# Attention and feed-forward kernel on one core: pooled value sums on TensorE for the first sequence, an earlier exp table, moved casts, ordered waits and a new plan

## Chip, cores and metric

One Trainium2 chip, one core. The metric is the device time of one execution in microseconds (us); of the kernel before, three runs were timed. A program of this kind is a set of five instruction streams that wait for each other through semaphores: TensorE (PE in the profile, its weight loads PEld), VectorE (DVE), ScalarE (ACT), GpSimd (POOL) and SyncE (SP), which here only issues transfers.

## What is computed

Eight sequences of 576 tokens, eight heads of 64. The reference, cut to what matters:

```python
def sm_attn(qq, kk, vv):                       # softmax(q k^T / 8) v
    s = scale * np.matmul(qq, kk.transpose(0, 1, 3, 2))
    a = np.exp(s - np.max(s, axis=-1, keepdims=True))
    return np.matmul(a / (np.sum(a, axis=-1, keepdims=True) + 1e-09), vv)
q_d, k_d, v_d = (mean over groups of 4 tokens of q, k, v)        # 144 pooled tokens
out_up = np.repeat(sm_attn(q_d, k_d, v_d), 4, axis=2)
out_local = the same attention over all 576 tokens, masked to |i - j| < 4
x = (out_up + out_local) as 4608 x 512
h = x @ w_in                                   # 512 x 2048
out = np.maximum(0.01 * h, h) @ w_out          # 2048 x 512
```

The products of the feed-forward part keep fp32 precision: each operand is split into a high and a low part of a shorter type (fp32r), and three matmuls (high by high, high by low, low by high) are summed.

## The kernel before

**Stages.** The 4608 tokens are cut into ten chunks of up to 512 columns. The first sequence is done on its own at the start, with its local attention on TensorE; the other seven sequences' local attention runs on POOL and DVE while TensorE works on the feed-forward products of the chunks that are there. Heads go in pairs, so a sequence has four channels c = 0 to 3 of 128 partitions.

- *Start, first sequence* (`pooled`, `vsums`, `vrest`, `windows`, `banded` with batch 0). Per channel: `given` loads q and k (qk); the pooled q and k (qk_d) are sums of four, by one DVE reduce (L525) or by two POOL additions (L519, L521; channels 1 and 2); TensorE multiplies them (L543), DVE takes the maximum (L555), ACT the exp (L561). `vsums` reduces the loaded v (su_vs) by four on DVE to su_vd (L445); L635 multiplies it with the weights. `banded` does the local part in two halves hf of the sequence (256 and 320 tokens): scores into a PSUM tile (L814), DVE maximum, subtraction and sum (L821, L822, L827), ACT exp (L825) and sum plus 1e-9 (L829), POOL scaling (L833), TensorE transposes (L841), ACT copy (L843), TensorE values (L856); DVE adds the pooled result, each column four times (L867), and ACT and DVE split the sum into x high and low (L879, L881). When all four channels of the first half are there, TensorE's feed-forward matmuls can begin.
- *Weights* (`convert`): every 128x512 piece of w_in and w_out is cast (L374 on ACT), repaired by a two-input DVE operation (L376), and split into high (L383 on ACT) and low (L386 on POOL or L389 on DVE, by a string of flags). It uses the prod tiles and, in the start, pieces of x1 (x in the rows).
- *Feed-forward*: `up_proj` (L1118, hp), `leaky` (ACT L1139 and L1140, DVE L1142: gh and gl), `down_proj` (L1164, acc). 
- *Other sequences*: per piece two POOL products of 128x1344 (scores L944, values L1020), each reduced by DVE (L950, L1026), then `landing` transposes and adds (L1042, L1050) into x. Pooled attention of these: `pooled` and `duo` (L688, L710).
- *Late chunks*: the last three are parked in DRAM and read back. `fetched`, `combine_x` and `split_t` read them into the output buffer (olot) and split or combine them with the two-input helper `both` (L1239); the last two chunks go through a Strassen scheme (`finale`, L1419).

**Order.** `Order` holds generators, each spawned with a rank. It repeatedly takes the operation that can start first by its own model of the engines (`COST`, a model of the transfers in `wire`), ties and near ties going by rank, and so writes the order of every engine's program, which then is fixed. Nothing overtakes on an engine. `staging`, `swap` and `cleared` open and close the buffers of the start; `busy` puts filler matmuls on TensorE where the plan has gaps (L342, L347, L355). `load` (L273) issues every transfer on SP.

**Two-input operations.** An operation of DVE with `lock` is planned behind what POOL has; `held` notes it, and `behind` adds a wait to a POOL operation that follows within 31.4 us of the plan:

```python
def held(ins):
    od.held = ins, od.engine["DVE"]
def behind(ins):
    first, end = od.held
    if first is not None and od.engine["POOL"] - end < NEAR:
        tc.add_manual_dep(ins.ins, first.ins.name, ...)
```

## Time and profile before

| | |
|---|---|
| median of three runs | 892.03 us (891.53 to 893.36) |
| the profiled execution | 893.24 us, its span 891.5 us |
| mean granted clock of TensorE | 0.993 |
| busy: PE, DVE, ACT, POOL | 872.8 us (98%), 639.4 (72%), 461.4 (52%), 628.9 (71%) |
| HBM traffic | 119.67 MB, 134 GB/s |
| chain that ended last | PE 86%, DVE 6%, DMA 4%, ACT 3% |

How to read it: the span is the profile's time from the first to the last record, the execution's own time lies 1.7 us around it. Busy shares are averages over stages; the view by stretches tells them apart. A row of the trace's groups gives line, engine, operation, tiles (out<-in), partitions x elements, xcount, the busy time and mean duration, and behind the last bar the idle time of the engine just before them with what ended it. In a timeline the columns are start, duration, engine, line, operation, and in brackets the idle time before it and what ended it.

### The profile page before, as it was taken

Reading aid. Unit: us, or ns where it says so; the run is one execution under the profiler, and the core shown is the slowest. Engines: PE = TensorE matmul, PEld = TensorE weight load, DVE = VectorE, ACT = ScalarE, POOL = GpSimd, SP = SyncE. Lnnn points to the kernel's source line nnn. Section 1 sums busy time; section 2 is a strip of 40 time slices with the busy share of each in tenths; the row PEclk is TensorE's granted clock in tenths of the full one; section 3 lists DMA queues with packets and bytes.
Section 4 is the critical chain, followed back from the end, with each engine's and each line's share of the span. In section 5 each row is a group of like instructions: output and inputs, shape, how many; then the busy total and the mean of one; then the engine's idle time right before and its main releaser. Section 6 shows DMA issues by size and latency. Waiting matters only on the chain.

```text
span 891.5 us, 13603 instructions
## 1 busy us (share of the span) xinstructions
PE 872.8 (98%) x4815; PEld 721.1 (81%) x4815; DVE 639.4 (72%) x952; ACT 461.4 (52%) x1288; POOL 628.9 (71%) x316
## 2 busy tenths in 40 slices
PE   6999999999999999999999999999999999999998
PEld 3687878988899888887888888778878888888886
DVE  5888989888896988898788977887786443323322
ACT  3898866656463744466345635623443244435421
POOL 3434478798999899999998899889976433374000
PEclk9999999999999999999999999999999999999999
DMA  9878764555453563455455535534344000000001
GB/s 336 278 234 293 241 187 133 191 167 186 140 154 111 180 189 113 139 160 171 119 148 174 171 107 160 158 100 116 115 113 137 3 24 24 1 1 1 24 24 48
DMA packets 67684, 119.67 MB, mean 134 GB/s; under 512 B 8608, under 2 KB 34720, under 8 KB 67616
## 3 DMA queue, kind: packets, MB, share of 16 engines
q1 hardware_dynamic: 67616, 118.80, 42.9%
q8 instruction: 38, 0.62, 0.3%
q14 instruction: 30, 0.25, 0.1%
HBM read 106.19 MB, written 12.58 MB: 133 GB/s over the span
## 4 chain that ended last, share of the span: by engine, by line
PE 86%; DVE 6%; DMA 4%; ACT 3%; issue 1%; SPq 0%; POOL 0%; DVEq 0%; POOLq 0%; ACTq 0%
PE acc L1164 35%; PE hp L1118 32%; PE hp L1419 4%; PE pt L1419 4%; DMA qk<-in_qkt_dram 3%; PE hp L1164 2%; PE pt L1164 2%; PE pt L688 1%; DVE xloc L1026 1%; PE pt L707 1%; PE pt L751 1%; DMA stage<-in_w_out_dram 1%; PE pt L710 1%; ACT x L374 1%; DVE gl L1142 0%
## 5 line engine op out<-in xcount | busy, mean ns | idle before, releaser
L1118 PE MATMUL hp<-x,wi 128*128 128x512 f32 (+2 forms) x1632 | 333.7, 356 | 4.1 <-DVE gl L1142 4.1
L1118 PEld LDWEIGHTS hp<-x,wi 128*128 128x128 f32 x1632 | 277.2, 189 | 45.6 <-DVE gl L1142 7.5
L1020 POOL TENSOR_TENSOR prod<-v,sx 128x1344 f32<-128x1344 f32 x84 | 264.3, 3148 | 29.3 <-DVE xloc L1026 16.8
L944 POOL TENSOR_TENSOR prod<-q,k 128x1344 f32<-128x1344 f32 x84 | 261.5, 3114 | 27.4 <-DVE wi L389 8.8
L1164 PE MATMUL acc<-woh,gh 128*128 128x512 f32 x512 | 202.4, 395 | 0.0
L1164 PE MATMUL acc<-wol,gh 128*128 128x512 f32 x512 | 199.9, 390 | 0.0
L1164 PE MATMUL acc<-woh,gl 128*128 128x512 f32 x512 | 199.8, 390 | 0.0
L1139 ACT ACTIVATE gh<-hp 128x512 fp32r<-128x512 f32 (+2 forms) x140 | 73.6, 526 | 143.5 <-PE acc L1164 130.2
L1026 DVE TENSOR_REDUCE xloc<-prod 128x192 f32<-128x1344 f32 x84 | 129.7, 1546 | 14.9 <-POOL prod L1020 14.5
L950 DVE TENSOR_REDUCE s<-prod 128x21 f32<-128x1344 f32 x84 | 129.2, 1538 | 9.7 <-POOL prod L944 9.3
L1142 DVE TENSOR_TENSOR gl<-hp,gh 128x512 fp32r<-128x512 f32 (+2 forms) x140 | 82.8, 594 | 58.5 <-ACT hp L1140 56.2
L1164 PEld LDWEIGHTS acc<-woh,gh 128*128 128x128 f32 x512 | 96.2, 188 | 20.6 <-issue 2.4
L1164 PEld LDWEIGHTS acc<-woh,gl 128*128 128x128 f32 x512 | 96.1, 188 | 20.7 <-DVE gl L1142 0.2
L1164 PEld LDWEIGHTS acc<-wol,gh 128*128 128x128 f32 x512 | 96.2, 188 | 18.0
L1140 ACT ACTIVATE hp<-hp 128x512 f32<-128x512 f32 (+2 forms) x140 | 72.9, 520 | 0.0
L1239 POOL TENSOR_TENSOR sl<-sr,sh 128x1024 fp32r<-128x1024 f32 x8 | 19.2, 2399 | 73.4 <-ACT sh L1243 73.4
L989 ACT COPY sx<-s 32x84 f32<-32x84 f32 x168 | 43.8, 261 | 11.9 <-POOL s L980 9.9
L1323 DVE TENSOR_TENSOR pt<-pt,sp 128x512 f32<-128x512 f32 x12 | 8.4, 699 | 56.4 <-PE pt L1419 31.0
L1050 DVE TENSOR_TENSOR pt<-pt,outd 128x128 f32<-128x128 f32 x126 | 40.1, 322 | 3.1
L445 DVE TENSOR_REDUCE v_d<-vs 128x128 f32<-128x512 f32 (+1 forms) x53 | 35.5, 670 | 5.6 <-DMA vs<-in_vrb_dram 4.4
L1239 DVE TENSOR_TENSOR gl<-wi,gh 128x512 fp32r<-128x512 f32 x14 | 9.7, 692 | 28.3 <-ACT gh L1243 28.3
L742 ACT ACTIVATE pd<-pd,st_d 112x144 f32<-112x144 f32 x72 | 24.5, 405 | 8.9 <-DVE st_d L739 8.8
(228 smaller groups left out, 1127.5 us busy)
## 6 DMA issues: line engine op xcount, KB each, us to landing
k<-in_kb_dram SPq DMA_DIRECT2D x84, 288.0 KB, 3.3
qk<-in_qkt_dram SPq DMA_DIRECT2D x32, 576.0 KB, 4.3
v<-in_vb_dram SPq DMA_DIRECT2D x84, 192.0 KB, 2.6
q<-in_qb_dram SPq DMA_DIRECT2D x84, 96.0 KB, 2.3
vs<-in_vmb_dram SPq DMA_DIRECT2D x28, 256.0 KB, 3.3
out_dram<-olot SPq DMA_DIRECT2D x28, 256.0 KB, 2.1
vs<-in_vrb_dram SPq DMA_DIRECT2D x28, 192.0 KB, 2.7
x<-in_w_out_dram SPq DMA_DIRECT2D x9, 511.8 KB, 6.4
```

What stands on the lines that cost most here:

```text
L944: behind(nc.gpsimd.tensor_tensor(out=prv, in0=q[:, :nj].unsqueeze(2).to_broadcast([128, nj, W, D]), in1=view(k, 0, [[D, nj], [D, W], [1, D]]),
L950: nc.vector.tensor_reduce(out=s[:, u, p, :nj], in_=prv, axis=AX.X, op=ALU.add)
L989: nc.scalar.copy(out=both[32 * g:32 * g + 32, :, h], in_=sv[src:src + 32])
L1020: behind(nc.gpsimd.tensor_tensor(out=prv, in0=view(v, 0, [[1, nj], [nv, ROWS], [1, W]]), in1=s[:, p].unsqueeze(2).to_broadcast([128, nj, R ...
L1026: nc.vector.tensor_reduce(out=xl_t[:, :nj, p], in_=prv, axis=AX.X, op=ALU.add)
L1050: nc.vector.tensor_tensor(out=part, in0=part, in1=view(outd[b], 2 * u * SD + o, [[2 * COLS // FAC, ROWS], [sm, cm], [sr, cr]]), op=ALU.add)
L1118: nc.tensor.matmul(hp[:, :n], w[h][:, ws], x[:, c], start=c + j == 0, stop=c == NC - 1 and j == 2)
L1139: nc.scalar.activation(out=gh[:, :n], in_=hp[:, :n], func=AF.Prelu, alpha=0.01)
L1140: nc.scalar.activation(out=hp[:, :n], in_=hp[:, :n], func=AF.Prelu, alpha=0.01)
L1142: nc.vector.tensor_tensor(out=gl[:, :n], in0=hp[:, :n], in1=gh[:, :n].bitcast(F32), op=ALU.subtract)
L1164: nc.tensor.matmul(acc, g[:, ts], w[h], start=f + j == 0, stop=f == NF - 1 and j == 2)
L1419: nc.tensor.matmul(acc, w[h][:, c * 128:(c + 1) * 128], T[x][m][:, c], start=c + j == 0 and name not in BEFORE, stop=c == 1 and j == 2, sk ...
```

## The change

- `FOURS`: in the first sequence the reduce by four of v (L445, four times) goes; L635 sums five products per head in PSUM in place of two, four of them on the four values of a pooled key (the fifth, as before, on the 16 pooled keys that `vrest` reduces).
- `PAIRED`: channel 0's pooled q and k also go to POOL (before 1 and 2 only).
- `SHIFTED`: channel 0's second half takes its exp straight from PSUM, in five ACT operations with bias and running sum, without DVE's subtraction and sum.
- `PLUS`: channel 2's first half adds the pooled result by one matmul in place of DVE's L867.
- `TOPPED`, `HIGHER`: five casts of the kind L374 and two of the kind L383 go from ACT to POOL; `LOWER`, `SUMMED`: one low part goes from POOL to DVE, other pooled sums of the later sequences change engine.
- `lit`: a memset and an exp of one column ahead of all, and with them the load of ACT's exp table.
- `both`: its DVE operations are noted by `held`, its POOL operations wait by `behind`.
- `swap` waits for the end of the fillers; `windows` of the second half waits for all four channels' v; a buffer of the end is set aside earlier; the planner's starts and its model of transfers change, and with them the fillers (first group 12 to 16, others 15 and 8 to 9 and 4), and some thirty ranks.

```diff
-LOWER = "01010101000100010000010000000000"
-SUMMED = "00000001000010000001"
+SHIFTED = "00001000"
+PAIRED = "1110"
+FOURS = "1111"
+PLUS = "00100000"
+TOPPED = "00000000000000110011000000000010"
+HIGHER = "00001000100000000000000000000000"
+LOWER = "01010101000100000000010000000000"
+SUMMED = "11100001000000000011"
...
-WARM, FILL, AGAIN, REST = 12, 29.404, 71.12, 0.38
+WARM, FILL, AGAIN, REST = 16, 31.881, 45.805, 0.38
...
-        t = yield from op("ACT", 600, t, s_u.t)
-        nc.scalar.copy(out=head.bitcast(F16).rearrange("p (m h) -> p m h", h=2)[:, :, 1], in_=top)
+        if TOPPED[2 * f + k] == "1":
+            t = yield from op("POOL", 256, t, s_u.t)
+            behind(nc.gpsimd.tensor_copy(out=high, in_=top))
...
+        if HIGHER[2 * f + k] == "1":
+            t = yield from op("POOL", 256, t)
+            behind(nc.gpsimd.tensor_copy(out=hi, in_=tf))
...
-            if c in (1, 2):
+            if PAIRED[c] == "1":
...
-                for v_k, p_k in ((v_i, pt_i[:, 0]), (left[0][rows], pt_i[rows, 1])):
+                parts = [v_i[:, :, :, r] for r in range(FAC)] if FOURS[c] == "1" else [v_i]
+                for k, v_k in enumerate(parts + [left[0][rows]]):
+                    p_k = pt_i[:, 0] if k < len(parts) else pt_i[rows, 1]
...
+        if SHIFTED[4 * hf + c] == "1":
...
+            nc.vector.tensor_reduce(out=mx, in_=spv, axis=AX.X, op=ALU.max, negate=True)
...
+            for i in range(nb):
+                nc.scalar.activation(out=sv[:, i], in_=spv[:, i], func=AF.Exp, scale=SCALE, bias=mx[:, i:i + 1], accum_out=sums[:, i:i + 1])
...
+        if plus:
+            te = yield from pe(n / 590, to, s_b.t)
+            nc.tensor.matmul(av[:, :n], id_sb, spread, start=True, stop=False, skip_group_check=True)
...
     def both(eng, out, in0, in1, alu):
-        (nc.vector if eng == "DVE" else nc.gpsimd).tensor_tensor(out=out, in0=in0, in1=in1, op=alu)
+        ins = (nc.vector if eng == "DVE" else nc.gpsimd).tensor_tensor(out=out, in0=in0, in1=in1, op=alu)
+        (held if eng == "DVE" else behind)(ins)
...
+nc.vector.memset(lit, 0)
+nc.scalar.activation(out=lit, in_=lit, func=AF.Exp)
...
     def swap():
         yield from wait("su", 3 * NC)
+        yield from wait("filled")
...
-        od.spawn(-46.661, cleared())
+        od.spawn(-119.87, cleared())
```

What the plan makes of it, at three places. Line numbers of the changed kernel are some 11 higher at L273, 17 at L374 and 44 to 46 from L879 on.

SP at the start, before (qk is a load of q and k, one per channel; su_vw, su_vr and su_vs are loads of v):

```order
L273 DMA su_vw<-in_vwb_dram 128x512 x2
L273 DMA qk_103<-in_qkt_dram 128x1152
L273 DMA su_vr<-in_vr_dram 128x512
L273 DMA idb_sb<-in_identb_dram 128x128
L273 DMA band_sb<-in_band_dram 128x630
```

and now:

```order
L284 DMA su_vw<-in_vwb_dram 128x512 x2
L284 DMA qk_106<-in_qkt_dram 128x1152
L284 DMA su_vr<-in_vr_dram 128x512
L284 DMA idb_sb<-in_identb_dram 128x128
L284 DMA band_sb<-in_band_dram 128x630
```

The first load of q and k stands behind the same two loads as before; nothing moved here.

ACT around the cast of the fourth channel's x, first half (L879 before; x is also the name of the weight pieces, acc that of the sum in PSUM), before:

```order
L374 CAST x_89<-prod 128x512
L609 COPY k<-pt 16x3x2x48
L383 CAST wi_79<-prod 128x512
L829 ACTIVATE lst<-lst 128x5
L843 COPY su_pt<-pt 70x512
L649 COPY outd<-pt 128x144
L383 CAST woh_88<-prod 128x512
L374 CAST x_89<-x_89 128x512
L879 CAST x_108<-acc_549 128x256
```

and now (L923 is that cast, L391 and L404 are the weight casts L374 and L383, L855 the new exps):

```order
L391 CAST x_89<-x_89 128x512
L923 CAST x_111<-acc_534 128x256
L404 CAST woh_88<-x_89 128x512
L391 CAST x_89<-prod 128x512
L852 ACTIVATE lst<-lst 128x5
L855 ACTIVATE xloc,lst<-pt,lst 128x70 x5
L923 CAST x_111<-acc_552 128x256
```

Ahead of the fourth cast stood eight L374 and seven L383; now eleven and eight of the kind, and the five exps of the second half, but neither the table load nor the exp of 350 columns. On DVE, ahead of the same x's low part, stand four L445, one L525, one L867, one subtraction, one sum and one reciprocal of the second half fewer, and three L376, one L389 and one reduce of a later sequence's v more.

DVE around the first reload (x from olot), before:

```order
L950 TENSOR_REDUCE s<-prod 128x21
L1142 TENSOR_TENSOR gl<-hp,gh 128x512
L1239 TENSOR_TENSOR x_6126<-olot,x_6126 128x512 x2
L1026 TENSOR_REDUCE xloc<-prod 128x6x32
L1142 TENSOR_TENSOR gl<-hp,gh 128x512
L1239 TENSOR_TENSOR x_6126<-olot,x_6126 128x512
```

and now:

```order
L1070 TENSOR_REDUCE xloc<-prod 128x6x32
L1186 TENSOR_TENSOR gl<-hp,gh 128x512
L1285 TENSOR_TENSOR x_6123<-olot,x_6123 128x512 x2
L994 TENSOR_REDUCE s<-prod 128x21
L1285 TENSOR_TENSOR x_6123<-olot,x_6123 128x512
L1070 TENSOR_REDUCE xloc<-prod 128x6x32
```

The pair still stands directly behind a gl and ahead of a reduce of a POOL product; the reduce behind it is now one of scores.

## Rows read from the trace of the kernel before

**Rows 1.** Stretches: length, busy PE, PEld, DVE, ACT, POOL, clock, DMA, GB/s.
```profile
0.00:38.90 38.90, 29.87 (x288) 17.12 (x288) 25.48 (x60) 23.62 (x66) 15.13 (x20) 0.96 0.89 321
38.90:250.00 211.10, 207.34 (x1439) 178.72 (x1438) 184.24 (x294) 146.78 (x457) 148.35 (x74) 0.98 0.62 197
250.00:560.00 310.00, 310.00 (x1659) 259.61 (x1658) 261.32 (x380) 162.88 (x511) 290.76 (x123) 1.00 0.50 150
560.00:887.60 327.60, 325.51 (x1435) 265.66 (x1433) 167.97 (x220) 127.81 (x255) 174.65 (x101) 1.00 0.19 56
```
**Rows 2.** The same view, two short stretches.
```profile
39.80:43.20 3.40, 3.40 (x41) 2.79 (x36) 2.58 (x5) 2.05 (x5) 1.13 (x4) 0.50 0.74 182
207.00:210.40 3.40, 3.40 (x30) 3.02 (x31) 1.79 (x3) 1.08 (x5) 3.40 (x2) 0.51 0.54 160
```
**Rows 3.** Timeline of PE: its longest waits after the start.
```profile
84.00 1.67 PE L1118 MATMUL hp<-x,wi 128*128 128x512 f32 x6 [1.40 <-DVE gl L1142]
...
206.92 0.43 PE L688 MATMUL pt<-qblk 64*64 64x144 f32 x2 [1.22 <-ACT outd L714]
...
580.39 1.42 PE L1118 MATMUL hp<-x,wi 128*128 128x512 f32 x5 [1.19 <-DVE gl L1142]
...
664.69 1.19 PE L1118 MATMUL hp<-x,wi 128*128 128x512 f32 x4 [0.89 <-DVE gl L1142]
```
**Rows 4.** The chain that ended last, in order of time, 0 to 50 us: start, us, what.
```profile
1.65 6.33 DMA qk<-in_qkt_dram
...
22.18 0.86 PE pt L635 x8
```
**Rows 5.** Timelines of ACT and PE around the fourth channel's x.
```profile
41.02 0.37 ACT L879 CAST x<-acc 128x256 fp32r<-128x256 f32 x1 [0.46 <-DVE acc L867]
...
44.37 1.31 PE L1118 MATMUL hp<-x,wi 128*128 128x256 f32 x9
```
**Rows 6.** Groups of DVE instructions, 8 to 43.7 us.
```profile
L376 DVE SCALAR_TENSOR_TENSOR x<-x 128x512 int32<-128x512 int32 x4 | 2.7, 682 | 0.0
L525 DVE TENSOR_REDUCE qk_d<-qk 128x288 f32<-128x1152 f32 x2 | 2.7, 1348 | 6.1 <-DMA qk<-in_qkt_dram 6.1
L445 DVE TENSOR_REDUCE su_vd<-su_vs 128x128 f32<-128x512 f32 x4 | 2.7, 670 | 0.0
...
L867 DVE TENSOR_TENSOR acc<-acc,outd 128x256 f32<-128x256 f32 x4 | 1.7, 420 | 0.5 <-PE acc L856 0.5
...
L822 DVE TENSOR_TENSOR xloc<-pt,lst 128x350 f32<-128x350 f32 x2 | 1.0, 522 | 0.2
```
**Rows 7.** Groups of ACT instructions, 12 to 41.4 us.
```profile
L561 ACT ACTIVATE v<-acc,st_d 128x144 f32<-128x144 f32 x12 | 4.6, 380 | 0.3
L374 ACT CAST x<-x 128x512 f16<-128x512 bf16 x5 | 3.7, 769 | 0.0
...
L561 ACT ACTIVATION_READ_ACCUMULATOR v<-acc,st_d 128x1 f32 x12 | 2.0, 163 | 0.0
...
L383 ACT CAST woh<-x 128x512 fp32r<-128x512 f32 x2 | 1.3, 652 | 0.0
L561 ACT ACT_TABLE_LOAD x1 | 1.3, 1283 | 12.1 <-DVE st_d L556 12.1
...
L825 ACT ACTIVATE xloc<-xloc 128x350 f32<-128x350 f32 x1 | 0.5, 497 | 0.6 <-DVE xloc L822 0.6
```
**Rows 8.** Groups of POOL instructions, 8 to 43.7 us.
```profile
L386 POOL TENSOR_TENSOR wol<-x,woh 128x512 fp32r<-128x512 f32 x2 | 2.6, 1298 | 0.0
L519 POOL TENSOR_TENSOR su_half<-qk 128x576 f32<-128x576 f32 x2 | 2.3, 1148 | 10.5 <-DMA qk<-in_qkt_dram 10.5
L521 POOL TENSOR_TENSOR qk_d<-su_half 128x288 f32<-128x288 f32 x2 | 1.3, 666 | 0.2
```
**Rows 9.** Reload: all DVE operations on olot (duration min/median/max), then timelines of DVE and POOL.
```profile
L1239 DVE TENSOR_TENSOR x<-olot,x x8: 676/1815/3602, 573.9 to 670.9; 128x512 fp32r<-128x512 f32 x8
...
573.93 4.34 DVE L1239 TENSOR_TENSOR x<-olot,x 128x512 fp32r<-128x512 f32 x2
...
574.15 3.57 POOL L944 TENSOR_TENSOR prod<-q,k 128x1344 f32<-128x1344 f32 x1
```

More of the change, by code (lines that the diff above doesn't have):

```diff
@@ L148, in __init__ @@
         self.released = {tag: [] for tag in bufs}
-        self.engine = dict.fromkeys(("PE", "DVE", "ACT", "POOL", "SP"), 0.0)
+        self.engine = dict(PE=2.0, DVE=1.0, ACT=3.5, POOL=1.0, SP=0.75)
         self.wire = 0.0
@@ L628, in pooled @@
         av = bank(s_b)
-        t = yield from pe(0.3 + 0.45 * n, s_b.t, *(x[5] for x in mine))
+        t = yield from pe(0.3 + 0.45 * n + (0.75 if b < BANDED and FOURS[c] == "1" else 0), s_b.t, *(x[5] for x in mine))
         for i, (_, _, _, pt_i, v_i, _) in enumerate(mine):
@@ L682, in duo @@
         s_2.free(0.0)
-        t = yield from pe(1.15, t, *(s.t for s in s_b))
+        t = yield from pe(1.0, t, *(s.t for s in s_b))
         for qi in range(3):
@@ L767, in windows @@
         if hf:
-            yield from wait(("vd", 0, c))
+            for p in range(NC):
+                yield from wait(("vd", 0, p))
         s_vw = yield from slot("su_vs" if hf else "su_vw")
@@ L864, in banded @@
         xv = av[:, :n].rearrange("p (s r) -> p s r", r=FAC)
[L865 to L869 removed]
+        if not plus:
+            t = yield from op("DVE", n, t, to)
+            nc.vector.tensor_tensor(out=xv, in0=xv, in1=spread, op=ALU.add)
+            od.signal(("read", b), t)
         od.signal(("held", b))
@@ L1046, in landing @@
         adds = ADDS[a, n]
-        t = yield from op("DVE", 128 * n + 115 * (len(adds) - 1), t, to, times=len(adds))
+        t = yield from op("DVE", 128 * n + 187 * (len(adds) - 1), t, to, times=len(adds))
         for (m, r, o), (dm, sm, cm), (dr, sr, cr) in adds:
@@ L1340, in first @@
             s_1.free(t)
-            od.spawn(-44.395, leaky(("g", 2 * p), EN, *held["B"], t))
+            od.spawn(-61.921, leaky(("g", 2 * p), EN, *held["B"], t))
         def rest():
```

112 lines of the change are left out of this document (67 added, 45 removed).

## Prediction

> **What bounds the kernel now.** I read the stretches first. TensorE is busy all the time from 38.9 us on, but for 211.10 - 207.34 = 3.8 us up to 250 and 327.60 - 325.51 = 2.1 us after 560 [rows 1]. Before 38.9 it has 38.90 - 29.87 = 9.0 us of idle time, and part of the rest is filler. DVE, ACT and POOL are each idle for a good part of every stretch [rows 1], so over the whole kernel none of them is the bound, and what the change can take is the start, 5.9 us of waits, and the time lost to TensorE's clock. That loss is in two stretches of 3.4 us at a granted clock of 0.50 and 0.51, which is the 1.2 GHz level; TensorE is busy throughout, so each costs about half its length, 1.7 us [rows 2]. I then looked up the waits in TensorE's timeline. Four make up 4.7 of the 5.9 us: 1.40 at 84, 1.22 at 207, 1.19 at 580 and 0.89 at 665 [rows 3]. The rest, 1.2, lies in small waits.
>
> The chain in order of time shows what the start is: the transfer of the first q and k lands 1.65 + 6.33 = 8.0 us in [rows 4], and from there it runs through DVE, ACT and TensorE in turns. It ends when the fourth channel's x is there: cast at 41.02, first matmuls on it at 44.37 [rows 5].
>
> The sums below are against the profiled execution, 893.24 us, which is 1.2 above the median of the runs, 892.03. I subtract that 1.2 at the end. What a measurement of this kernel can tell from no change is about 0.2%, 1.8 us.
>
> **Term 1, the start: 0, between -2.1 and +3.9.** The words of the change promise the first q and k ahead of all, but SP's order has it in the same place, behind two loads: nothing. Where the fourth channel's x is made, two engines count.
>
> - DVE loses four L445 of 0.670, one L525 of 1.348, one L867 of 0.420, and a subtraction and a sum of 350 columns, both priced as L822 at 0.522: 2.68 + 1.35 + 0.42 + 1.04 = 5.5. It gains three L376 of 0.682, one L389 that I price as those, and one reduce of a later v at L445's 0.67: 3.4 [rows 6]. Net -2.1 us.
> - ACT gains three L374 of 0.769, one L383 of 0.652, and five exps with the read of their sums. The nearest row is the exp of 144 columns, 0.380 and 0.163 for its read; 70 columns cost no more, and at least the read: 0.8 to 2.7 for five. It loses the table load, 1.283, which now runs while everything waits for q and k, and one exp of 0.497. Net 2.31 + 0.65 + 2.7 - 1.78 = +3.9 at most, +2.0 at least; I take +3.6, near the row that the exps resemble [rows 7].
>
> ACT has 38.90 - 23.62 - 12.1 = 3.2 us of idle time behind its first exp [rows 1, 7], and 0.46 more just ahead of the last cast [rows 5]. If the work that was added falls into that idle time, DVE sets the end and the start is 2.1 shorter; if none does, the cast is 3.9 later, and so are its matmuls. The likeliest is that half of it fits, +1.8 on ACT's side against -2.1 on DVE's, and I write 0. The table load is 1.283 us, and ahead of all twelve exps that follow lie 0.3 us of idle time together [rows 7]. The Trainium skill ("ScalarE: Activation LUTs", What ACT_TABLE_LOAD costs) gives the same 1283 ns but adds a drain of some 1380 ns; by that ACT would have 1.4 us more to give, and the rows show no room for such a drain.
>
> Costed at nothing: the three more products per channel on TensorE. The two products per head take 0.86 us for a channel, 0.43 each [rows 4], so three more are 1.3 us per channel and 5.2 for four; they lie in TensorE's 9.0 us of idle time and fillers [rows 1]. If the last channel's lies on the chain, 1.3 are lost, inside the range above. Channel 0's pooling on POOL is 1.148 + 0.666 = 1.8 for DVE's 1.35, 0.5 later for that channel [rows 6, 8]; POOL is idle for over half of the start [rows 1]. PLUS's matmul replaces L867 for one channel; on TensorE I price it as one such product, 0.43, for DVE's 0.42.
>
> **Term 2, seven casts on POOL: 0.** No row has a cast on POOL. It costs between ACT's 0.652 [rows 7] and POOL's two-input subtraction of the same width, 1.298 [rows 8]; most of the seven follow after 38.9, where POOL is busy for 148 of 211 us [rows 1]. At most 0.65 x 7 = 4.5 us more of POOL's time, in which it has over 60 idle. Only if a weight piece is then late does TensorE wait; that is in term 5.
>
> **Term 3, the wait at 84: -0.7, between -1.4 and +1.4.** This leaky waits behind the conversion of the first weights that are loaded after the start's buffers are closed. The new order closes them earlier by fewer fillers, but also makes that wait for the fillers' end. Between losing the 1.40 [rows 3] and doubling it nothing decides; I take half of it as a gain.
>
> **Term 4, reloaded x: -2.1, between -2.1 and 0.** The DVE halves of a reloaded chunk take 0.676 us when alone and up to 3.602 [rows 9]. The pair at 573.93 takes 4.34, and a POOL product runs from 574.15 for 3.57: it ends at 577.72, and the second half, which would have been done at about 575.3, ends at 578.27. So DVE stood still behind POOL for some 3 us. The gl queued behind it came late, and TensorE waited 1.19 and 0.89 at the two reloads [rows 3]. With the halves held, POOL's product waits instead. POOL is no bound there: 174.65 busy of 327.60 [rows 1]. What would be late next is the reduce of that product, by one DVE half or two, 0.7 to 1.4. The order of the changed kernel still has the pair directly behind a gl, so the next gl is late by 1.4 at most instead of 4.3. I take both waits as gone.
>
> **Term 5, the new order between 200 and 250, and new waits: -0.8, between -2.9 and +4.** The wait of 1.22 at 207 is followed at once by one of the two half-clock stretches, so the two go together: 1.22 + 1.70 = 2.9 [rows 2, 3]. The changed ranks move pooled attention and its loads against the feed-forward work. Half of it as a gain is -1.5. The new order will have waits of its own: the old one has 1.2 us of small ones, and I add 0.7 for others, up to as much as all of its waits apart from the reloads, 3.8 [rows 1].
>
> **Sum.** 0 + 0 - 0.7 - 2.1 - 0.8 = -3.6. 893.24 - 3.6 = 889.6, and on the scale of the median 888.4 us.
>
> **Rivals.**
>
> *A. The start gains too* (0.17). ACT's added work falls into its idle time, term 1 is -2.1, and the clock's half-speed stretch at 207 goes with its wait, -1.4 more: 888.4 - 3.5 = 884.9. For it: DVE's list gets shorter, and the idle time of 3.6 is as long as what ACT gains at +3.6. Against: the casts must stand in the right place, and ACT's order shows the five exps directly ahead of the fourth cast.
>
> *B. No change* (0.21). The held halves don't do what they say: a hold binds only a POOL operation that follows in the plan, within 31.4 us of it. A product that already runs when the pair starts is as before, and DVE is blocked as long as before. Then term 4 is 0, and with new waits of 2.2 in place of 0.7 the sum is 0 + 0 - 0.7 + 0 + 0.7 = 0: 892.0. For it: at 573.93 the pair starts ahead of the product by 0.2 only, and its second half is what stands still [rows 9]; against: that is exactly the case that the wait covers.
>
> *C. ACT becomes the bound of the start* (0.14). The five exps and three more casts ahead of the fourth cast find no idle time: +3.9. TensorE, idle in the meantime, has one more half-clock stretch like that at 39.8 [rows 2]: +1.7. Terms 3 to 5 give -3.6 as before, so the sum is 3.9 + 1.7 - 3.6 = +2.0: 895.2 for the profiled execution, 894.0 on the median's scale. Its place is the cast L923 of the fourth channel. Delay and clock together must pass 3.6 us before the gains are eaten: a cast at 43 us or later, if the clock falls too, at 44.6 if it doesn't.
>
> *D. POOL and DVE block each other more than before* (0.06). Seven casts on POOL beside the two-input operations of DVE that convert the weights. The pair of the reload lost 3.0 us to a product of 3.57 [rows 9], 0.84 of its length; by that, seven casts of up to 1.298 [rows 8] hold DVE for up to 7.6 us. If half of it comes ahead of a gl or an x that TensorE waits for, that is +3.8, and with term 3 at +1.4 in place of -0.7 the sum is -3.6 + 3.8 + 2.1 = +2.3: 894.3. Against it: `behind` makes a cast wait for the DVE operation that was noted last, and DVE's work on later weights has room [rows 1]. The Trainium skill ("SBUF — State Buffer", SBUF: two separate sides) says of DVE's and GpSimd's shared port pair that whichever starts first has it for its whole instruction. The reload's rows agree: 3.602 against 0.676.
>
> **Chances and range.** The forecast, 888.4 with 886 to 890, has 0.42. With A it makes 0.59 for faster; of C and D, 0.20, some 0.17 is slower by over 0.2% (above 893.8) and 0.03 joins B's 0.21, so no change has 0.24. The range is to hold 8 in 10: from 884.5, which takes in A but for its best outcomes, to 894.2, the middle of C and the lower part of D.
>
> **What would show it.** The fourth channel's cast L923 before or after 41.0, and its first matmuls against 44.37. The table load ahead of 8 us. L1285 on DVE at about 0.7 us each and no wait of TensorE on gl next to it. No half-clock stretch near 207. If the first matmuls on the fourth channel come at 46 or later, term 1 was wrong; if L1285 still takes over 3 us, term 4; if TensorE's idle time between 38.9 and 560 is above 4 us, terms 3 and 5.

## The result and the profile after

The changed kernel takes 898.19 us (median of four, 897.36 to 898.66), the kernel before, timed beside it, 891.78 (891.08 to 893.36, four). The ratio is 1.0068 with a 95% interval of 1.0051 to 1.0086: slower by 0.0068 x 891.78 = 6.1 us, where 3.6 us less were forecast, and outside the range. Ratios here and below are taken over all runs, so they differ a little from the quotient of two medians. The profiled execution of the changed kernel took 897.85 us, its span is 896.1; TensorE's last matmul ends 4.6 us later than before.

The stretches of the changed kernel (columns as in [rows 1]; the last one ends with TensorE's last matmul), then four short ones:

```profile
0.00:38.90 38.90, 31.53 (x295) 21.01 (x296) 21.07 (x52) 23.83 (x66) 16.95 (x22) 0.87 0.86 310
38.90:250.00 211.10, 203.54 (x1412) 174.32 (x1411) 178.59 (x281) 133.98 (x419) 152.86 (x81) 0.99 0.60 189
250.00:560.00 310.00, 309.79 (x1668) 258.20 (x1667) 256.04 (x379) 165.40 (x522) 275.23 (x116) 1.00 0.49 147
560.00:892.20 332.20, 331.61 (x1490) 272.26 (x1488) 172.43 (x235) 135.48 (x287) 187.89 (x107) 1.00 0.22 64
...
10.00:16.00 6.00, 6.00 (x60) 4.16 (x57) 3.73 (x11) 2.58 (x11) 3.79 (x6) 0.54 1.03 413
33.00:36.00 3.00, 3.00 (x22) 2.16 (x19) 2.97 (x7) 2.64 (x7) 1.30 (x1) 0.50 0.49 118
90.50:94.00 3.50, 3.50 (x16) 3.17 (x15) 2.09 (x5) 2.41 (x6) 0.91 (x1) 0.51 1.04 386
...
207.00:210.40 3.40, 3.40 (x27) 2.63 (x26) 2.00 (x3) 1.84 (x4) 3.40 (x3) 1.00 0.65 208
```

Against [rows 1, 2], one stretch improved as forecast: after 560 TensorE is idle for 332.20 - 331.61 = 0.6 us, before 2.1. The half-clock stretches at 39.8 and 207 are gone. But between 38.9 and 250 it is idle for 7.6 us, before 3.8, and the clock falls elsewhere: to 0.54 at 10 to 16, 0.50 at 33 to 36 and 0.51 at 90.5 to 94.

How far TensorE has come is read from the busy time that it still has ahead of it, from 60 us and from 110 us on; the third line is the stretch of the old wait at 207 (columns: length, busy PE, clock, DMA, GB/s). The kernel before:

```profile
60.00:900.00 840.00, 821.78 (x4320) 1.00 0.40 123
110.00:900.00 790.00, 773.32 (x3992) 1.00 0.38 113
200.00:250.00 50.00, 48.37 (x303) 0.97 0.53 162
```

The changed kernel:

```profile
60.00:900.00 840.00, 826.62 (x4338) 1.00 0.40 122
110.00:900.00 790.00, 779.95 (x4035) 1.00 0.38 113
200.00:250.00 50.00, 49.40 (x308) 1.00 0.53 159
```

At 60 us the changed kernel has 826.62 - 821.78 = 4.8 us more ahead of it, at 110 us 6.6. Behind 110 its TensorE is idle for 2.0 us less (892.20 - 110 - 779.95 = 2.3 against 887.60 - 110 - 773.32 = 4.3), and 4.6 remain. So the loss is made in the start and just behind it. TensorE's longest waits there:

```profile
46.53 2.04 PE L1162 MATMUL hp<-x,wi 128*128 128x256 f32 x12 [1.70 <-ACT x L923]
...
49.99 0.95 PE L1162 MATMUL hp<-x,wi 128*128 128x256 f32 x6 [0.97 <-DVE gl L1186]
...
90.16 2.58 PE L1162 MATMUL hp<-x,wi 128*128 128x256 f32 x12 [2.37 <-DVE gl L1186]
```

The fourth channel's first matmuls start at 46.53, before at 44.37 [rows 5], behind a cast at 46.09 instead of 41.02. ACT's timeline shows that cast, and further down the stop behind which the wait at 90 forms:

```profile
41.20 0.78 ACT L391 CAST x<-x 128x512 f16<-128x512 bf16 x1 [0.98 <-DVE acc L912]
41.84 0.37 ACT L923 CAST x<-acc 128x256 fp32r<-128x256 f32 x1
42.10 0.71 ACT L404 CAST woh<-x 128x512 fp32r<-128x512 f32 x1
43.67 0.78 ACT L391 CAST x<-prod 128x512 f16<-128x512 bf16 x1 [0.87 <-DMA prod<-in_w_out_dram]
...
44.60 0.32 ACT L855 ACTIVATE xloc<-pt,lst 128x70 f32<-128x70 f32 x1
...
46.09 0.39 ACT L923 CAST x<-acc 128x256 fp32r<-128x256 f32 x1
...
86.70 0.80 ACT L391 CAST x<-stage 128x512 f16<-128x512 bf16 x1 [2.50 <-DMA stage<-in_w_out_dram]
```

The five exps and their reads lie directly ahead of the fourth cast, 46.09 - 44.60 = 1.5 us. That looks like the cause, and they do delay that cast. But ACT stands idle for 0.98 and 0.87 just before, and the delay is older: the second channel's x is cast at 33.66 (before 30.19), the third's at 41.84 (34.10). DVE's timeline shows why the second is late:

```profile
27.89 0.69 DVE L466 TENSOR_REDUCE v_d<-vs 128x128 f32<-128x512 f32 x1 [1.72 <-DMA vs<-in_vmb_dram]
28.50 0.43 DVE L865 TENSOR_REDUCE lst<-xloc 128x4 f32<-128x280 f32 x1
28.85 0.61 DVE L580 TENSOR_REDUCE acc<-acc 128x3 f32<-128x432 f32 x1
...
32.14 0.68 DVE L466 TENSOR_REDUCE v_d<-vs 96x128 f32<-96x512 f32 x1 [0.51 <-DMA vs<-in_vrb_dram]
32.75 0.42 DVE L912 TENSOR_TENSOR acc<-acc,outd 128x256 f32<-128x256 f32 x1
```

L466 is the reduce of the *next* sequence's v. It waits 1.72 us for its transfer, and the first sequence's sum (L865), maximum (L580) and pooled addition (L912) are queued behind the two. In the kernel before, the same reduces stand later and wait for nothing:

```profile
27.86 0.44 DVE L827 TENSOR_REDUCE lst<-xloc 128x4 f32<-128x280 f32 x1
...
29.22 0.60 DVE L555 TENSOR_REDUCE acc<-acc 128x3 f32<-128x432 f32 x1
...
33.98 0.67 DVE L445 TENSOR_REDUCE v_d<-vs 128x128 f32<-128x512 f32 x1
...
43.57 0.67 DVE L445 TENSOR_REDUCE v_d<-vs 96x128 f32<-96x512 f32 x1
```

The load of this v was no faster there: issued at 18.39, it took 8.2 us. How the wait reaches the second channel is seen on ACT: its addition needs the copy of the pooled result (outd), which in the changed order stands behind three exps of a later channel, and these need the maximum L580. The copy before, then now:

```profile
26.54 0.27 ACT L649 COPY outd<-pt 128x144 f32<-128x144 f32 x1
...
31.11 0.32 ACT L676 COPY outd<-pt 128x144 f32<-128x144 f32 x1
```

POOL's scaling is late as well in the changed kernel, last released by a weight repair on DVE that `behind` makes it follow:

```profile
31.17 0.66 POOL L871 TENSOR_TENSOR xloc<-xloc,lst 128x280 f32<-128x280 f32 x1 [3.69 <-DVE x L393]
```

SP issues that v at 19.02, and it is there 8.8 us later, while the page's row for these loads gives a median of 2.9 us (KB each, then us from issue to landing):

```profile
vs<-in_vmb_dram SPq DMA_DIRECT2D x28, 256.0 KB, 2.9
```

### The profile page after: what moved, and what is told of

Same layout as the page of the kernel before. It is cut to its first block, busy times and chain, and to the rows that moved or that the text cites. A ratio compares the mean times of both kernels' runs of the same rounds, so it can differ in the third digit from the quotient of the medians.

```text
span 896.1 us, 13741 instructions
## 1 busy us (share of the span) xinstructions
PE 876.5 (98%) x4859; PEld 725.8 (81%) x4859; DVE 628.6 (70%) x946; ACT 459.1 (51%) x1292; POOL 632.9 (71%) x324
## 3 DMA queue, kind: packets, MB, share of 16 engines
q1 hardware_dynamic: 67616, 118.80, 42.8%
## 4 chain that ended last, share of the span: by engine, by line
PE 78%; POOL 4%; DMA 4%; DVE 3%; issue 3%; ACT 2%; SPq 0%; POOLq 0%; ACTq 0%; DVEq 0%
PE acc L1208 33%; PE hp L1162 28%; PE pt L1466 6%; DMA qk<-in_qkt_dram 2%; PE hp L1208 2%; PE pt L1208 2%; PE hp L1466 2%; POOL prod L988 2%; POOL prod L1064 2%; PE pt L715 1%; PE pt L778 1%; PE pt L734 1%; PE pt L737 1%; DMA vs<-in_vrb_dram 1%; DMA q<-in_qb_dram 1%
## 5 line engine op out<-in xcount | busy, mean ns | idle before, releaser
L1162 PE MATMUL hp<-x,wi 128*128 128x512 f32 (+2 forms) x1632 | 337.8, 356 | 6.9 <-DVE gl L1186 4.8
L1183 ACT ACTIVATE gh<-hp 128x512 fp32r<-128x512 f32 (+2 forms) x144 | 76.0, 528 | 159.2 <-PE acc L1208 138.5
L1186 DVE TENSOR_TENSOR gl<-hp,gh 128x512 fp32r<-128x512 f32 (+2 forms) x144 | 85.3, 595 | 43.1 <-ACT hp L1184 42.8
L1184 ACT ACTIVATE hp<-hp 128x512 f32<-128x512 f32 (+2 forms) x144 | 75.3, 523 | 0.0
L466 DVE TENSOR_REDUCE v_d<-vs 128x128 f32<-128x512 f32 (+1 forms) x53 | 35.5, 670 | 7.6 <-DMA vs<-in_vrb_dram 5.6
L1364 ACT COPY sp<-pt 128x512 f32<-128x512 f32 x24 | 14.1, 587 | 37.9 <-PE pt L1466 35.9
L1370 DVE TENSOR_TENSOR hp<-hp,sp 128x512 f32<-128x512 f32 x24 | 16.7, 700 | 21.5 <-ACT sp L1364 21.2
```

The costliest lines, as they stand in the source:

```text
L1162: nc.tensor.matmul(hp[:, :n], w[h][:, ws], x[:, c], start=c + j == 0, stop=c == NC - 1 and j == 2)
L1183: nc.scalar.activation(out=gh[:, :n], in_=hp[:, :n], func=AF.Prelu, alpha=0.01)
L1184: nc.scalar.activation(out=hp[:, :n], in_=hp[:, :n], func=AF.Prelu, alpha=0.01)
L1186: nc.vector.tensor_tensor(out=gl[:, :n], in0=hp[:, :n], in1=gh[:, :n].bitcast(F32), op=ALU.subtract)
```

## The experiments

Eighteen kernels, each timed beside the kernel before on the same chip. "The changed order" means that the planner's choice is replaced by a written list of the order that it chose, so that a single edit can't reshuffle the rest; lines are then 98 higher than in the changed kernel.

**Whole parts.** First the hold alone in the kernel before, order unchanged:

```diff
-    (nc.vector if eng == "DVE" else nc.gpsimd).tensor_tensor(out=out, in0=in0, in1=in1, op=alu)
+    ins = (nc.vector if eng == "DVE" else nc.gpsimd).tensor_tensor(out=out, in0=in0, in1=in1, op=alu)
+    (held if eng == "DVE" else behind)(ins)
```

> The kernel before with only the notes and waits in the two-input helper; every engine's order is as before. If term 4 is right by itself: DVE's halves of the reloaded x take about 0.7 us each, the waits of 1.19 and 0.89 us at 580 and 665 go, and the time is 1.5 to 2.5 us shorter than before. Rival: the waits return at the reduces behind the held products, no change.

Measured: 887.48 us, ratio 0.9958 (0.9944 to 0.9973): faster by 3.7 us. Its stretch after 560:

```profile
560.00:884.00 324.00, 323.93 (x1430) 264.86 (x1429) 157.51 (x217) 126.60 (x253) 169.53 (x100) 1.00 0.19 56
```

and its reloaded halves (duration min/median/max):

```profile
L1239 DVE TENSOR_TENSOR x<-olot,x x8: 679/684/2408, 572.9 to 665.3; 128x512 fp32r<-128x512 f32 x8
```

The median half fell from 1815 ns [rows 9] to 684 (the longest of the eight still takes 2408), and 0.07 us of idle time is left of 2.1. The reverse, the changed kernel without the hold (`both` as in the lines with a minus above, order unchanged):

> The changed kernel without the notes and waits in the two-input helper; the order of every engine is the same. If the waits are what removed TensorE's waits at the two reloads, DVE's halves take up to 3.6 us again, the two waits of about 1.2 and 0.9 us come back, and the time is 2 us longer, 900 us. If the new order did it, it stays at 898 us.

Measured: 903.55 us, 1.0145 (1.0106 to 1.0185), above the changed kernel by 5.4 us by the medians and 6.9 by the ratios, where 2 were expected. In its stretches 560 to 620 and 620 to 700 TensorE is idle for 3.8 us each:

```profile
560.00:620.00 60.00, 56.24 (x258) 44.92 (x257) 45.28 (x59) 26.95 (x81) 45.88 (x22) 1.00 0.42 123
620.00:700.00 80.00, 76.22 (x334) 62.12 (x333) 61.10 (x71) 30.27 (x75) 67.00 (x27) 1.00 0.35 100
```

and its median half is back at 2800 ns:

```profile
L1285 DVE TENSOR_TENSOR x<-olot,x x8: 679/2800/3602, 590.2 to 691.8; 128x512 fp32r<-128x512 f32 x8
```

where in the changed kernel it takes 694:

```profile
L1285 DVE TENSOR_TENSOR x<-olot,x x8: 678/694/2392, 592.2 to 686.6; 128x512 fp32r<-128x512 f32 x8
```

So the hold does what it says, in both orders. What else the change brings must therefore lose 10 to 13 us: 3.7 + 6.1 = 9.8 with the hold in both kernels, 0.0145 x 891 = 12.9 without it in either.

Next the plan alone, then the parts alone:

```diff
-WARM, FILL, AGAIN, REST = 12, 29.404, 71.12, 0.38
+WARM, FILL, AGAIN, REST = 16, 31.881, 45.805, 0.38
...
-    od.spawn(71.075 + 10 * b + a + 0.5 * u, landing(i, b, j0, u, a, z, col, s_x, xl_t, t, k == len(lands) - 1))
+    od.spawn(190.653 + 10 * b + a + 0.5 * u, landing(i, b, j0, u, a, z, col, s_x, xl_t, t, k == len(lands) - 1))
...
```

That is the edit of plan_alone, with the other ranks, the planner's starts and its model of transfers; parts_alone undoes the same lines in the changed kernel.

> The kernel before with the new ranks, planner starts, transfer model and fillers, but with none of the other parts. Theory N: most of the loss is here, 896 to 899 us. Theories O and P: 890 to 893 us, since the five exps and the further products are missing.

> The changed kernel's parts with the old ranks, starts, transfer model and fillers. Theory P: 895 us or more, since the further products are there. Theory N: 889 to 892 us. Theory O: 890 to 893 us, for here the five exps stand 13 rows ahead of the fourth cast and not directly before it.

Measured: 912.39 (1.0235, 1.0202 to 1.0268) and 902.39 (1.0125, 1.0095 to 1.0156). Either is worse than both together. So ranks and parts depend on each other, and such a pair of runs doesn't split the loss.

Therefore the parts were put into the old order: first the exp table, then the casts on POOL, then `LOWER` and channel 0 of `PAIRED` too.

```diff
# hold_table = hold_alone, and
+nc.vector.memset(lit, 0)
+nc.scalar.activation(out=lit, in_=lit, func=AF.Exp)
...
# hold_casts = hold_alone in the kernel before's order, and
+TOPPED = "00000000000000110011000000000010"
+HIGHER = "00001000100000000000000000000000"
...
# four_parts = hold_casts, hold_table, and
-LOWER = "01010101000100010000010000000000"
+PAIRED = "1110"
+LOWER = "01010101000100000000010000000000"
```

> The same, and the exp of one column ahead of all that brings the table's load forward. The load of 1.28 us leaves the chain at 12 us. If the start is a chain in which ACT's first exp counts, another 0.5 to 1.3 us shorter than with the waits alone; if later transfers set the start, the same as with the waits alone.

> The kernel before in its own order with the waits in the two-input helper and the seven casts on POOL at the same places of the order. Beside 887.5 for the waits alone: the same within 1 us, since ACT's idle time ahead of the fourth cast takes what the casts give back; if POOL's casts wait for DVE's noted operation and hold the products behind them, 1 to 2 us longer.

> The order of the kernel before with those parts of the change that fit into it one for one: the waits in the helper, the early table, the seven casts on POOL with the low part back on DVE, and channel 0's pooling on POOL. If these parts are harmless and the order is what costs, 886 to 889 us, as with the waits alone (887.5). If casts and pooling on POOL are what costs, 890 us or more.

Measured: 887.22 (0.9956, 0.9939 to 0.9973), 888.08 (0.9959, 0.9945 to 0.9974) and 887.66 (0.9954, 0.9937 to 0.9970). None differs from hold_alone by more than the intervals allow (0.0015 to each side, 1.3 us), though in the profiled executions of hold_table and four_parts the first leaky starts at 42.8, in hold_alone's at 45.09: an earlier start alone brought nothing that could be measured. The table load is in fact out of the way in the changed kernel (L1495 on ACT's timeline):

```profile
0.74 1.28 ACT L1495 ACT_TABLE_LOAD   x1 [0.74 <-PEq L1620]
```

and the casts on POOL cost 0.64 us (L401) and 1.00 (L388), by the groups of the changed kernel:

```profile
L388 POOL CAST x<-x 128x512 f16<-128x512 bf16 x4 | 4.0, 1004 | 3.2 <-issue 2.1 <-ACT hp L1184 0.9 <-DMA x<-in_w_in_dram 0.2
...
L401 POOL CAST wi<-x 128x512 fp32r<-128x512 f32 x1 | 0.6, 637 | 2.2 <-DVE x L393 2.2
```

So in the old order these parts neither cost nor gain anything measurable beside the hold. The 10 us lie in what is left: `FOURS`, `SHIFTED`, `PLUS`, the changed `SUMMED`, the fillers, the further waits of `swap` and `windows`, and the new order.

**Is it ACT, as rival C has it?** In the changed order the fourth cast, and the low part behind it, were moved ahead of the weight cast, the scale and the five exps; the five exps were undone; then both.

```diff
# pin_cast, ACT (DVE's low part L1023 likewise)
+L1021 CAST x_111<-acc_552 128x256
 L489 CAST x_89<-prod 128x512
 L950 ACTIVATE lst<-lst 128x5
 L953 ACTIVATE xloc,lst<-pt,lst 128x70 x5
-L1021 CAST x_111<-acc_552 128x256
...
# no_five_exps
-SHIFTED = "00001000"
+SHIFTED = "00000000"
...
# cast_no_exps = pin_cast and no_five_exps
```

> The changed kernel with every engine's order written out as the plan made it, and one piece moved: the fourth channel's cast of x and DVE's low part of it stand ahead of the weight cast that waits for its transfer at 43.7 us, of the scale and of the five exps. Theory O (the order on ACT delays the fourth channel): its first matmuls come at about 44 us in place of 46.5, the last values of the first sequence and with them the load of the next weights 2 to 3 us earlier, time 894 to 896 us. Theory P (the three more products per channel take TensorE's own time, so that an earlier cast only queues): 897.5 to 898.5 us, no change. Theory N (the new ranks in general, later than the start): under 1 us gained.

> The changed kernel in its own order, with DVE's subtraction and sum and one exp in the five exps' place. Theory O (ACT's queue ahead of the fourth cast and of the first leaky): the cast comes at about 44.5 in place of 46.1, the first leaky at 47 in place of 48.6, time 1 to 2 us shorter than the changed kernel's, 896 to 897 us beside 891.8 of before. Theory P (the further products): no change, 898 us.

> The changed kernel in its own order with both edits tried singly before: the fourth cast and its low part moved ahead of the weight cast, and one exp, a subtraction and a sum in the five exps' place. Theory Q (several things stand in a row ahead of TensorE's first feed-forward work, each a little shorter than the next, so that one removed gains nothing): the fourth channel's matmuls at 43 to 44 us and the first leaky at 46 to 46.5 in place of 48.6, 2 to 3 us shorter than the changed kernel, 895 to 896 us where that has 898. Rival R (the transfers of the weights set the start): the first leaky stays at 48 or later, no change.

Measured: 898.89 (1.0075, 1.0050 to 1.0100), 898.31 (1.0072, 1.0058 to 1.0085), 898.19 (1.0076, 1.0056 to 1.0096). The fourth cast came at 42.7 to 43.2 instead of 46.09, and no time was gained that could be measured: the first leaky on ACT stayed at 48.0 to 48.6. The last thing seen ahead of a late cast was not what set the time.

**Is it the added products or the casts?**

```diff
# two_products; three_undone = this and cast_no_exps
-parts = [v_i[:, :, :, r] for r in range(FAC)] if FOURS[c] == "1" else [v_i]
+parts = [v_i[:, :, :, r] for r in range(1)] if FOURS[c] == "1" else [v_i]
...
# casts_on_act
-TOPPED = "00000000000000110011000000000010"
-HIGHER = "00001000100000000000000000000000"
+TOPPED = "00000000000000000000000000000000"
+HIGHER = "00000000000000000000000000000000"
```

> The changed kernel in its own order, but with only one of the four values of each pooled key multiplied; the other three are left out of the sum, so that TensorE has two products per head as before. Theory P: TensorE's 3.4 to 5 us of further products are gone and the first sequence's x comes earlier, 3 us or more shorter than the changed kernel, 895 us or less. Theory O: the products lie in waits for ACT, under 1 us shorter, 897.5 us or more.

> The same, and only one of the four values of each pooled key multiplied (the other three are left out of the sum). Theory Q: another 0.5 to 1.5 us shorter, 894 to 895.5 us. Rival R: no change against the changed kernel.

> The changed kernel in its own order, the seven casts on ACT again at the same places of the order. If the move of the casts is a gain at the start, where one of 0.64 us stands ahead of the fourth cast, the fourth cast comes 0.6 later and the time is 0.5 to 2 us longer, 899 to 900 us. Rival (POOL's casts hold up DVE or wait for it themselves, as the 2.2 and 7.0 us ahead of two of them in the trace): the weights come earlier, 1 us or more shorter.

Measured: 898.34 (1.0073, 1.0057 to 1.0090), 896.73 (1.0054, 1.0038 to 1.0070), 899.37 (1.0083, 1.0062 to 1.0105). All three intervals overlap that of the changed kernel, so neither the added products nor the casts on POOL are shown to cost anything.

**Is it the order behind the cast?** The first two leakies were moved ahead of weight casts, without and with the five exps, and in the last the third channel's chain ahead of weight conversions.

```diff
# order_mended = pin_cast, and on ACT (DVE: gl ahead of the low part L508)
-L502 CAST woh_88<-prod 128x512
 L965 ACTIVATE lst<-lst 128x5
 L961 ACTIVATE xloc<-xloc 128x350
+L1281 ACTIVATE gh<-hp 128x256
+L1282 ACTIVATE hp<-hp 128x256
...
+L502 CAST woh_88<-prod 128x512
...
# leaky_first = order_mended with SHIFTED all zeros
# chain_first = order_mended, and on ACT
-L489 CAST x_89<-x_89 128x512
 L774 COPY outd<-pt 128x144
+L489 CAST x_89<-x_89 128x512
```

> The kernel with the fourth cast ahead and one exp in the five exps' place, and now the first two leakies on ACT ahead of two weight casts (the high part of a weight piece, which waited 1.23 us for DVE, and the next piece's cast), DVE's low part of that piece behind the two gl. Theory S (the first feed-forward work stands on ACT behind weight casts that wait for their transfers): TensorE's wait of 3.03 us at 49.85 shrinks to under 0.7, the first leaky comes at 46 to 46.5 in place of 48.6, and the time is 2 to 3 us shorter than without this move, 895 to 896 us. Rival T (the weight pieces are needed just as soon): the wait moves to a product on the delayed piece, under 1 us gained.

> All parts of the change kept, with only its order mended at the start: the fourth cast and the first two leakies moved as before. Theory S: the first leaky at 47 in place of 48.6, 1 to 2 us shorter than the changed kernel, 896.5 to 897.5. Rival T: no change, 898 us.

> All parts of the change kept, its order mended further: besides the fourth cast and the first two leakies, the third channel's copy, sum, cast and low part stand ahead of the weight conversions (three on DVE, three on ACT) that were between them in the last 2.5 us of its chain. If the start is late because short steps of the first sequence stand behind weight conversions, the third cast comes at 39.5 to 40.5 in place of 41.8, the first leaky at 45 to 46 in place of 48.6, and the time is 2 to 3 us shorter than the changed kernel's 898. If it is late for what comes before (the second channel at 33.7 where it was at 30.2), the third and fourth casts move by under 1 us and the time stays within 1 us.

Measured: 899.42 (1.0094, 1.0064 to 1.0125), 896.46 (1.0065, 1.0041 to 1.0090), 899.22 (1.0088, 1.0069 to 1.0107). In order_mended's profiled execution, the fastest of its six (893.50), the first leaky starts at 45.14, earlier than before (45.72); over all six the time is not clearly below the changed kernel's. chain_first brought the third cast to 39.99, as expected, and no time. In none of the six kernels with a moved cast did the second channel's x come before 32.0 us; in the kernel before it came at 30.19. So a common delay lies ahead of everything moved so far.

**The waiting reduce.** Only the two reduces of the next sequence's v are moved, and on SP the second one's load with it; the first load keeps its place on SP.

```diff
# vsum_late, DVE
-L564 TENSOR_REDUCE v_d<-vs 128x128
 L963 TENSOR_REDUCE lst<-xloc 128x4
...
-L564 TENSOR_REDUCE v_d<-vs 96x128
 L1010 TENSOR_TENSOR acc,outd 128x256
...
 L1023 TENSOR_TENSOR x_111<-acc,x_111 128x256
+L564 TENSOR_REDUCE v_d<-vs 128x128
...
# vsum_mended = vsum_late and order_mended
```

> The changed kernel's own order, in which only the two partial sums of the next sequence's v (L466 of the changed kernel, at 27.89 and 32.14 us there, waiting 1.72 and 0.51 us for their transfers) stand later on DVE, the first behind the fourth channel's low part. If those two waiting instructions hold the first sequence's channels up, the x of the second channel is cast by 31 to 32 us (33.7 in the changed kernel), the third by 38.5 to 40 (41.8), the fourth by 43.5 to 45 (46.1), the first matmuls on gh start at 46 to 47 (48.6), and the time is 895 to 896.5. If the transfers of the weights and values set the start, the casts may come earlier, but gh stays at 48 or later and the time is that of the changed kernel, 898 within 1.

> The same, with the moves of order_mended besides: the first two leakies on ACT ahead of two weight casts, gl ahead of one low part, the fourth cast and its low part ahead of the weight's cast, the scale and the five exps. If the order of the start alone makes the changed kernel slower, both together come near the start of the kernel before: first gh at 45 to 46, the last values of the second half by 76 to 78, and 893 to 895.5. If the loss lies in the order further on, or in the granted clock, the start is earlier and the time stays at 896 to 898.

Measured: 895.04 (1.0044, 1.0028 to 1.0059; nine runs) and 893.50 (1.0028, 1.0014 to 1.0043; eight). In vsum_late's DVE timeline the sum and the maximum stand 2.6 us earlier (28.50 and 28.85 in the changed kernel). Of this, 0.8 is there at the first channel's cast already, ahead of everything that was moved (the granted clock from 8 to 16 us was 0.57 in the changed kernel's profiled execution and 0.79 in this one, which may be why). The move itself is worth 1.8. The last two rows come further down:

```profile
25.91 0.45 DVE L963 TENSOR_REDUCE lst<-xloc 128x4 f32<-128x280 f32 x1 [0.50 <-ACT xloc L961]
26.27 0.61 DVE L678 TENSOR_REDUCE acc<-acc 128x3 f32<-128x432 f32 x1
...
89.94 0.68 DVE L564 TENSOR_REDUCE v_d<-vs 96x128 f32<-96x512 f32 x1 [2.09 <-DMA vs<-in_vrb_dram]
90.55 0.68 DVE L1284 TENSOR_TENSOR gl<-hp,gh 128x512 fp32r<-128x512 f32 x1
```

TensorE's waits near them, and the stretch:

```profile
87.25 1.70 PE L1260 MATMUL hp<-x,wi 128*128 128x256 f32 x12 [1.90 <-DVE gl L1284]
...
91.28 4.09 PE L1260 MATMUL hp<-x,wi 128*128 128x512 f32 x21 [1.63 <-DVE gl L1284]
```

```profile
38.90:250.00 211.10, 201.98 (x1383) 173.56 (x1383) 180.95 (x283) 134.48 (x422) 155.27 (x81) 1.00 0.59 188
```

Where the casts and the first leaky start, in us, from ACT's timelines, and how long the two reduces of the next sequence's v waited for their transfers together. The first gh needs all four channels; feed-forward matmuls on the first ones start earlier (at 38.93 in the kernel before).

| | 1st channel | 2nd | 2nd behind 1st | waits of the reduces | 3rd | 4th | first gh | ratio |
|---|---|---|---|---|---|---|---|---|
| before | 25.01 | 30.19 | 5.18 | 0 | 34.10 | 41.02 | 45.72 | 1 |
| changed | 24.50 | 33.66 | 9.16 | 2.23 | 41.84 | 46.09 | 48.58 | 1.0068 |
| no_five_exps | 24.25 | 32.06 | 7.81 | 0.89 | 40.73 | 43.22 | 48.56 | 1.0072 |
| leaky_first | 24.49 | 33.92 | 9.43 | 2.97 | 43.03 | 44.09 | 48.85 | 1.0094 |
| cast_no_exps | 24.13 | 33.78 | 9.65 | 2.76 | 42.06 | 42.87 | 48.60 | 1.0076 |
| order_mended | 23.56 | 32.64 | 9.08 | 2.39 | 40.16 | 41.35 | 45.14 | 1.0065 |
| vsum_late | 23.74 | 31.10 | 7.36 | 0 | 39.28 | 43.13 | 45.61 | 1.0044 |
| vsum_mended | 23.28 | 30.62 | 7.34 | 0 | 38.37 | 39.35 | 43.37 | 1.0028 |

In the eleven kernels of the changed order with the two reduces in their place, these wait 0.89 to 2.97 us and the second cast follows the first by 7.8 to 9.7, by and large the later the longer they wait; with the reduces moved it is 7.3 to 7.4. So it is the waiting that costs, more than the reduces' own 0.69 and 0.68, and how long it is differs from execution to execution. In time, moving the reduces is worth 0.0024 x 891 = 2.1 us (1.0068 to 1.0044; the two intervals overlap a little) and, with the moves of order_mended in both kernels, 0.0037 x 891 = 3.3 us (1.0065 to 1.0028, with hardly any overlap). From the changed kernel to vsum_mended it is 3.6 us, and the intervals are apart. So the waiting reduces were one cause. What the moves of order_mended add is not shown: 0.0003 without this edit, 0.0016 with it, both within the intervals.

It is not the whole loss: vsum_mended is still 0.0070 above hold_alone, 6.2 us. Three things are left, and no kernel here took one of them alone. First, the second cast still follows the first by 7.3 us where it was 5.2, and the third the second by 7.8 to 8.2 (3.9 before); in vsum_late the copy of the second channel's pooled result still stands behind three exps, at 28.54. Second, vsum_mended has its fourth cast and its first gh earlier than the kernel before, and is still slower than it by 0.0028, 2.5 us: part of the loss lies behind the first gh. In vsum_late's profile TensorE is idle for 9.1 us between 38.9 and 250, in hold_alone's for 4.2. Third, the DVE rows at 90 show one more instance of the same thing, a reduce of v that waits 2.09 us with a gl behind it, and TensorE waits 1.63 at 91.28 for that gl. ACT stops for the next weights just before 84 in vsum_late and just before 87 in the changed kernel. Those are issued late, at 78.90 (changed kernel 81.41, before 75.32); in both kernels of the changed order that is 0.88 us behind the last values of the first sequence's second half, at 78.02 and 80.53 (before 72.36). That this makes up the rest was not tried.

No kernel of the changed order beat the kernel before. The version that beats both is the kernel before with the hold alone, 0.9958.

## Why the prediction was wrong, step by step

**Term 4, the reload: right in its mechanism, and undersized.** Forecast -2.1, and no more than that. TensorE's waits there went as forecast; hold_alone gained 3.7 (2.4 to 5.0), and without the hold the changed kernel lost 5.4 to 6.9. Of the 3.7, some 2.0 is the idle time after 560. Where the other 1.7 comes from is open. In hold_alone's profiled execution the half-clock stretch at 207 is missing, which is as much; but the mean clock of its six runs, 0.9968, and of those of the kernel before beside them, 0.9964, differ by too little for more than 0.4 us. I had tied that stretch to the wait of 1.22 and put it into term 5. The wait is still there in hold_alone (1.27).

**Term 1, the start: the step that failed.** It says "one reduce of a later v at L445's 0.67". The row's duration was right (0.69), its price was not: it waits 1.72 us for its transfer, and with it the first sequence's sum, maximum and addition, which are queued behind it. I counted which instructions stand ahead of the *fourth* cast and added their durations. On engines that run in order the question is, for every row that is moved ahead, when its input arrives. The DMA share of 0.89 in the start [rows 1] was a warning that it may arrive late, and the trace of the kernel before had the number: the same load took 8.2 us there, from 18.39 to 26.6. Here what delayed the second channel delayed the later ones too; a sum over the fourth can't see it. The term was to lie between -2.1 and +3.9; the fourth cast came 5.1 later, its first matmuls 2.2, at 46.53 and so past the text's own mark of 46, and the first gh 2.9. The reduces explain 1.8 of the 4.0 us that the changed kernel loses up to the second cast (9.16 against 5.18) and 2 to 3 us of the time; what else in the new order holds the channels up stays open. The added products, costed at nothing, cost nothing that two_products could show.

**Rival C had the sign, not the mechanism, and its place was luck.** It named the fourth cast at 43 or later with one more half-clock stretch. The cast came at 46.09; of the half-clock stretches two went (39.8, 207) and others came (10 to 16, 33 to 36, 90.5 to 94), and the mean clock stayed, 0.992 against 0.993. That the five exps are the cause is refuted: with them gone or behind the fourth cast, this came 3 us earlier and the time stayed. That ACT's further weight casts cost nothing is not shown; order_mended moved two of them behind the first leaky without a clear gain, and no kernel took them away. **Rival A**'s condition, an earlier start, was not met.

**Term 3, the wait at 84: the wrong sign.** Forecast -0.7, +1.4 at most. In its place stands a wait of 2.37 at 90.16, 1.0 more, and 3.5 us at a clock of 0.51 behind it, worth another 1.7: +2.7 in all. The clock's part may be chance: in vsum_late, with waits of 1.90 and 1.63 there, the clock doesn't fall. The text priced the fillers' end but not that the second half's channels would be late, with the next weights issued 6.1 us later instead of earlier.

**Term 5: right where it looked, and its new waits came elsewhere.** Between 200 and 250 TensorE's idle time fell from 1.6 to 0.6 us and the clock rose from 0.97 to 1.00, together some 2.5 where half of 2.9 was forecast; the clock's part of this is partly luck, as the last section shows. The new waits, "I add 0.7 for others", are 3.8 us more idle time than before between 38.9 and 250. All of them lie ahead of 110 us, at the places of terms 1 and 3 (1.70 and 0.97 behind the fourth cast, 2.37 at 90); from 110 to 250 there is 0.7 us less. The text's own mark, above 4 us between 38.9 and 560, was passed with 7.8. The bound, as much as all of the old waits, was itself no bound: a new order may wait more than the old one.

**Term 2, casts on POOL: right.** hold_casts equals hold_alone within the intervals, and the casts took 0.64 to 1.00 us on average, in or just under the range of 0.65 to 1.30. **Rival B** (the hold doesn't work) and **rival D** (POOL and DVE block each other in the start) find no support: hold_casts is no slower than hold_alone, casts_on_act no faster than the changed kernel, and the reload's halves are back at 0.69.

## What to carry to other kernels

Price an instruction that moves ahead on an in-order engine by when its input arrives, and then by everything queued behind it; its own duration counted least here. The old trace often has the landing time of that input already. When a stage is a chain of channels, look for the first channel that is late: edits at the last one can move its cast by 3 us and the time by nothing. A planner's table of ranks and the operations it orders are one thing: swap in either alone and both looked worse (1.0235, 1.0125) than the pair (1.0068), so put each part into the *old*, written-out order to see what it is worth.

## What the runs showed of the hardware that was not expected

A drop of TensorE's clock behind a wait did not come with every execution of the same wait. In five kernels of the old order the same wait of 1.22 to 1.28 us stands near 204 to 207. In three of these profiles the clock fell behind it, to a mean of 0.72 (before, 206 to 212 us), 0.72 (hold_table, 202 to 208) and 0.74 (hold_casts, 206 to 212); in hold_alone and four_parts it stayed at 1.00 from 202 to 212. The row of before, then that of hold_alone:

```profile
206.00:212.00 6.00, 5.08 (x39) 4.70 (x40) 3.04 (x4) 3.11 (x12) 5.43 (x2) 0.72 0.68 214
```

```profile
206.00:212.00 6.00, 5.03 (x46) 4.51 (x47) 3.89 (x7) 3.48 (x14) 5.44 (x2) 1.00 0.77 227
...
206.90 0.34 PE L688 MATMUL pt<-qblk 64*64 64x144 f32 x2 [1.27 <-ACT outd L714]
```

TensorE is about as idle in both (0.92 and 0.97 us of 6). So one execution's half-clock stretch of 1.7 us is partly luck, and a forecast that counts on losing it counts on too much. hold_alone's six runs differ in the same way, 886.5 to 887.1 at a mean clock of 0.998 and 887.9 to 889.5 at 0.995 to 0.996; but the clock is not all: runs of the kernel before at 0.998 went from 888.9 to 893.5.

Whether variants of the changed order scatter more isn't settled: order_mended's six runs went from 893.5 to 900.2 and leaky_first's from 894.7 to 904.2, hold_alone's only from 886.5 to 889.5, but the changed kernel's own four lay within 1.3 us, and the kernel before, timed beside all of these, went from 888.8 to 894.9.
